# Batch 3's residual turned by transposing transfers instead of TensorE, with every step of the kernel in a new order

## The chip, the cores and the metric

The kernel runs on one core of a Trainium2 chip. The metric is the time of one execution in microseconds (us) on the device. A core has TensorE (PE in the profile; its weight loads are PEld), VectorE (DVE), ScalarE (ACT), GpSimd (POOL) and SyncE (SP), which here issues all transfers that the kernel asks for. Each engine runs its own instructions in the order in which they were written, and waits for others by semaphores.

## The reference

Eight batches of 576 positions, 8 heads of 64 channels. An attention part makes x from q, k and v, and a mixing part makes the output from x. Cut to what is computed:

```python
# attention: two terms, added
q_d, k_d, v_d = means over 4 neighbouring positions        # 576 -> 144 positions
out_up = repeat(softmax(q_d @ k_d.T / 8) @ v_d, 4)          # coarse, all 144 x 144
mask = abs(i - j) < 4
out_local = softmax(where(mask, q @ k.T / 8, -1e9)) @ v     # fine, a band of 7
x = (out_up + out_local), heads side by side                # (8, 576, 512)
# mixing
theta = x @ w_theta
zr, zi = x * cos(theta), x * sin(theta)
y = w_tok_r @ zr + w_tok_i @ zi                             # over positions
u = x + y
return u + maximum(u @ w_ch, 0)                             # (8, 576, 512)
```

## The kernel before

All matmuls are in bfloat16 with sums in float32. The work of a batch is cut into small steps, each a Python function of a batch and a piece, with a two-letter name. `ORDER` is a string of 1223 words written out ahead of time; the kernel goes through it and emits one step for each word. The first two letters name the step, the rest says where it goes: PSUM banks as digits for TensorE's steps, an engine for copies (`v` VectorE, `a` ScalarE, `g` GpSimd), a staging buffer for loads. The batch and the piece are not in the word: every step takes its next one from a fixed sequence (`STEPS`). After each word `pin()` ties every new instruction to the one before it on the same engine, so the words are the order of each engine's queue, and of SP's.

One batch goes like this. Loads of q and k (`lq`, `lk`) and of v (`lv`, `lw`, two halves of a chunk) go into 14 staging buffers `st`; `cq`, `ck`, `cv` cast them. TensorE turns q and k (`tp`, line 304) and `ev` (317) evicts them to `qT`, `kT`. `kd`, `qd` (323, 331 and on) make the coarse sums. `ps` (483), `ex` (491), `mk` (502), `po` (512), `nm` (520, 521) are the band: scores, exponentials, the mask, products with v, division. `sd` (427), `ed` (438), `pv` (405), `vd`, `nd` (448, 453), `xn` (458, 459), `xd` (467), `xc` (471) are the coarse part. `xt` (531) turns the band's result and `xa` (537) adds both into `xT`, which holds x with channels on the partitions.

`th` (548) multiplies 128 positions of x by `w_theta`, `cs` (553, 554) takes cosine and sine, `tt`, `ct` (560, 565, 566) do so for the last 64 positions. `xm` (587) turns x back for `zz` (594), which makes z; `zt` (569) with `zp`, `zc` or with the transfer `dz` (573) makes the tail of z. `mx` (610) is the mixing over positions, nine matmuls for one piece of 128 channels by 288 positions, and there are eight pieces to a batch; `ua` (615) adds x and gives `uT`. `ch` (635) multiplies by `w_ch`, `rl` (640) takes the maximum with zero and adds the residual `ur`, which is u with positions on the partitions, and `st` (644) stores. `ut`, `dt` (647), `ht`, `rt` (656) and the stores at 661 do the last 64 positions for two batches at a time.

The weight over positions comes in by `lb`, `cb`, is turned by `wp` (275) and copied to `WT` by `wc` (279); no `mx` can run before the last `wc`. `wm` words put matmuls on zeros into TensorE's queue (715). `te` and `ts` switch ScalarE's table between exponential and sine (720).

The residual `ur` is made in one of two ways. For the batches in `RPE` TensorE transposes it, `up` (624), and `uc` (627) copies it out of PSUM. For the others four transposing transfers `du` (619) do it, one for each block of 128 channels, on SP's queue and into the same buffer:

```python
def du(b, dc, w):
    nc.sync.dma_start_transpose(out=ur[b % 2][:, :, P * dc:P * dc + P], in_=uT[b % 2][:, dc, 0:512])
def up(b, c, w):
    ps = at["up", b, c] = bank16(w)[:, 0:DM]
    for dc in range(4):
        nc.tensor.transpose(out=ps[:, P * dc:P * dc + P], in_=uT[b % 2][:, dc, P * c:P * c + P], identity=ident)
def uc(b, c, w):
    COPY[w](out=ur[b % 2][:, c, :], in_=at.pop(("up", b, c)))
```

`uT`, `ur`, `xT`, `z` exist twice, and a batch takes the one of its parity.

Of the kernel before, what the change touches and what calls it, by code (L numbers as in the profile page):

```python
# [58 lines left out]
cqg lq7 lk8 lk9 tp45 cqg kcg kcg x12 lqa eva lqb kdg cvv kca cka wm62 tp67 lkc x13 lkd cvv eva ckv wm13 pv01 cqv lq0  # L59
la2 cqg lb1 tp45 qdv eva wm22 tp23 eva wm65 ps67 kdg vdv lq3 qdv ckg cka ps45 cag ex wm25 sd23 ex lb4 ed cbg lk5 sd01  # L60
cqg ps67 mkv ed po45 nm po23 nd45 nd01 la6 nm la7 xn xn lk8 mkg tp23 cag po45 ex xt6 po01 cqa eva la9 lqa mkg caa xd7
lqb ckg xca ckg nm tp23 nm xt4 xt5 lbd cag lbc cbg lb2 xt7 xa cqg lb1 eva lb0 cbg lb3 lb6 tp01 xa po23 th4 xa xm5 xa
lv7 cqg nm cbg th6 lw xt7 cbg th2 lv5 xm3 evv cbg ts cs tp01 lv8 lv9 cs cbg xa tt4 zz cs xm5 wp6 wp2 zz lw lw wp3 lw
lv4 lw cbg lqa zz ct lqd eva qdg ztv wp7 cba th4 wcv zp5 lkb xm6 wcv lkc kdg wcv wp2 wp3 wcv zcv wp0 wcv wp1 cs wp7
wca wcv ps45 lk2 lk1 wcv wcv ps23 te ex qdg ps01 lq0 zz kdv cva ex mx7 mx6 mx4 cvg ua sd23 cvg cvg mkv lc3 ex po01 ua
sd67 ed ed mkv mx5 ua nm po23 ua po01 cvg pv67 nm nm mkg vda mx4 ua po23 lq6 cqg po67 nd01 nm nd45 mx2 up3 xn lq7 ckg
xn cqg lk5 cka nm tp01 xd4 lk8 up5 uca eva xcv xt3 ucv lk9 tp67 cka xt4 xt0 ua ckg xt1 kdg lv4 xa xa xa mx5 xa eva lva
tp23 ua th4 xt0 lw xa evv cqg th5 xm1 lvb lcd lqc tt0 lw lk1 lv2 lv0 lw ts cs lw xm4 cqg cs tp67 ckg cqg th2 xm3 th5
ct lw cka zz tp01 cs qdg zz cs xm2 evv ztg lc6 lc5 zp4 mx6 ccg zz qdg zcv zz eva cvg mx7 ps45 te ex ua ps23 ua ckg kdv
ex mkv ps01 mx6 lq7 mx7 po45 sd23 ex lq8 lk3 kdg ed cvg sd01 cqg ckg ua lk4 lq9 mx6 tp23 mkv lva lw lvc lw nm ua tp45  # L70
up7 cvg mkv cvv ed mx0 eva cvg pv23 ccg ua ucv eva po67 po45 ua nm up1 nm vda ccg ccg ch0 nd67 lq1 xn nd23 lkb cqg cqa
tp45 uca qdg xn mx1 xd2 xt3 eva ps67 rl lq0 ua po45 xcv kdg qdg ps01 ch2 xa ckg ex mkg nm rl mx3 ps67 cqg lv2 cka po45
ex ua sd01 lkd xt2 ckg ex nm mx3 xt4 xt5 xa up2 ua cqa cqg tp67 cvv ed up3 xa evv uca th0 xa lv6 xt1 up2 xa lw th4 xm6
ucv ts cs uca th5 cvg lq5 ckg po01 cvg zz cs nm po23 xm7 cs ch6 nm tt4 tp01 lw ct tp23 th5 rl mkg ch4 lq7 zz st eva
evv rl po67 sd01 cs cqg cvg ztg po23 ch5 nm nm rl ch4 lv8 lw te ed cvg st pv67 vda zp0 zca lk4 cka lk3 lk1 tp23 cqa
mkg ckg lq9 lqb rl qdg lva lw xm1 eva ckg utg lv0 zz lw xm5 ch4 nd67 lvc zz xn lw nd01 mx5 lvd xn mx6 st ps23 rl lv2
ua po01 kdg nm ps45 ua mx7 lk5 ex xd0 cqa xt1 ex up6 ua xcv ucv lk6 kdv tp23 cqg utg mx0 tp45 qdg xa ua eva sd67 xt2
lv8 xt3 ch1 eva xa mkg ed xa th0 mkv rl cvg lk3 lw xt6 xt7 xa xa lw lk1 cvg th2 mx1 ua ts cs xm3 cvg tt0 zz th6 st lq4
cs cvg cka po45 dt cvg ckg ct po23 th7 mx1 ztg lk7 cs lvb nm pv45 cs ckg po67 cqg kdg lw nm ua sd23 mx0 cvg nm te ed
zp1 tp67 vdv zcv ht2 tp45 xm1 rt lw ua lq9 mx3 eva zz ps67 eva ua lva qdg po45 nm ex ps01 lq0 ex xm2 up3 zz lqc nd67  # L80
uca lvd tp45 cqa xm2 qdg xn nd01 zz mx3 cka cka xn mx2 xd0 up1 lk2 lv6 kdg st ua mx3 cqa mkv lw uca xcv eva tp67 xt0
up1 lk5 ua ua cva ucv xt4 xa mx5 st xa st eva ps23 mkg sd01 qdg po67 lw ed ua nm lv3 xt4 mx5 xt6 cva mx7 po01 ua ex
# [675 lines left out]
```

## Time and profile before

| | |
|---|---|
| Time, median of 3 runs | 236.6 us (235.68 to 238.39) |
| The profiled execution | 236.41 us, its span 234.7 us |
| Mean granted TensorE clock | 0.997 |
| Busy: TensorE, its weight loads | 223.5, 155.7 us |
| Busy: VectorE, ScalarE, GpSimd | 187.6, 159.7, 143.9 us |
| HBM read, written | 33.98, 9.44 MB |
| Start of the first `mx` | 40.62 us |

Everything below is from that one execution. Its span runs from the first to the last instruction, 1.7 us less than the time. A busy TensorE is not TensorE at its peak: the ends of its matmuls are modelled, so small waits can hide in busy time. In a group's row stand the line, the engine, what it writes and reads, the shapes, the count, then busy us and the mean ns of one, and the idle time ahead of it with what ended it. In the order of time stand the start, the duration and the instructions merged there.

### The profile page before, as it was taken

The page shows a single profiled execution, that of the slowest core. Times are in us where ns is not written, and L with a number is a line of the kernel's source. Part 1 is how long each engine was busy: PE and PEld are TensorE (multiplying, and loading weights), DVE is VectorE, ACT ScalarE, POOL GpSimd, SP SyncE. Part 2 cuts the span into 40 slices and gives each one's busy share as a digit, 9 for nine tenths or more (in the row PEclk, how much of TensorE's full clock was granted, in tenths as well). Part 3 has the DMA queues.
Part 4 walks back from the last instruction along what each step waited for, and adds up shares of the span by engine and source line. Part 5 has one row for each costly group of instructions (what it writes and reads, how often), then busy time and mean ns, then how long its engine had stood idle before and what let it go on. Part 6 is the DMA issues. An engine that isn't in the chain of part 4 may idle for free.

```text
span 234.7 us, 8524 instructions
## 1 busy us (share of the span) xinstructions
PE 223.5 (95%) x3500; PEld 155.7 (66%) x3500; DVE 187.6 (80%) x377; ACT 159.7 (68%) x239; POOL 143.9 (61%) x190
## 2 busy tenths in 40 slices
PE   7998899999999699999999999899999999999992
PEld 3555767687787466786688757676676665577740
DVE  5169997999898689888799869969898879466472
ACT  2389898669987779869987796859889358510000
POOL 7858999809999995983874628794598310100000
PEclk9999999999999999999999999999999999999998
DMA  6999979996959999999986206996967357674477
GB/s 196 383 392 386 287 163 276 391 244 143 290 162 250 243 345 212 224 224 244 287 183 173 61 0 141 292 236 139 127 155 169 73 124 197 91 221 109 110 226 244
DMA packets 76647, 49.35 MB, mean 210 GB/s; under 512 B 61120, under 2 KB 61120, under 8 KB 76608
## 3 DMA queue, kind: packets, MB, share of 16 engines
q1 hardware_dynamic: 76608, 48.81, 81.4%
q8 instruction: 27, 0.44, 0.8%
q14 instruction: 12, 0.10, 0.2%
HBM read 33.98 MB, written 9.44 MB: 185 GB/s over the span
## 4 chain that ended last, share of the span: by engine, by line
PE 85%; DVE 8%; issue 3%; DMA 2%; ACT 1%; SPq 0%; DVEq 0%
PE PS L610 29%; PE PS L635 12%; PE PS L548 10%; PE PS L304 5%; PE PS L531 3%; PE PS L512 3%; PE PS L715 3%; PE PS L587 2%; PE PS L483 2%; DMA z<-zT 2%; PE PS L275 2%; DVE tmp L521 2%; PE PS L448 2%; PE PS L624 2%; PE PS L652 1%
## 5 line engine op out<-in xcount | busy, mean ns | idle before, releaser
L610 PE MATMUL PS<-WT,z 128*128 128x288 bf16 x576 | 77.9, 286 | 0.4 <-DMA z<-zT 0.4
L610 PEld LDWEIGHTS <-z 128*128 128x128 bf16 x576 | 54.3, 98 | 16.0 <-DMA z<-zT 0.7
L615 DVE TENSOR_TENSOR uT<-PS,xT 128x288 bf16<-128x288 f32 x64 | 28.8, 452 | 12.4 <-PE PS L610 11.9
L548 PE MATMUL PS<-wth,xT 128*128 128x512 bf16 x128 | 32.2, 379 | 0.0
L635 PE MATMUL PS<-wch,uT 128*128 128x512 bf16 x128 | 31.1, 379 | 0.0
L569 POOL TENSOR_TENSOR zT<-xT,cst 128x512 bf16<-128x512 bf16 x7 | 8.1, 1153 | 35.9 <-ACT cst L566 27.6
L521 DVE TENSOR_TENSOR tmp<-PS,rl 128x512 bf16<-128x512 f32 x40 | 27.6, 691 | 1.4
L502 POOL TENSOR_TENSOR pm<-pm,band 128x1024 bf16<-128x1024 bf16 (+1 forms) x14 | 25.1, 1792 | 5.5 <-ACT pm L491 5.5
L537 DVE TENSOR_TENSOR xT<-PS,xdT 128x464 bf16<-128x464 f32 (+1 forms) x40 | 24.0, 628 | 4.5 <-PE PS L531 2.3
L640 DVE SCALAR_TENSOR_TENSOR osb<-PS,ur 128x512 f32<-128x512 f32 x32 | 21.8, 684 | 5.2 <-PE PS L635 4.9
L491 ACT ACTIVATE pm<-PS 128x1024 bf16<-128x1024 f32 (+1 forms) x24 | 20.4, 880 | 6.4 <-PE PS L483 6.4
L553 ACT ACTIVATE cs<-PS,pihc 128x512 bf16<-128x512 f32 x32 | 22.1, 692 | 3.0 <-PE PS L548 2.8
L331 POOL TENSOR_TENSOR two<-kT 128x580 f32<-128x580 bf16 x13 | 15.0, 1154 | 9.4 <-ACT kT L317 6.6
L720 ACT ACT_TABLE_LOAD x15 | 19.2, 1283 | 0.3
L635 PEld LDWEIGHTS <-uT 128*128 128x128 bf16 x128 | 11.9, 98 | 11.1
L554 ACT ACTIVATE cs<-PS 128x512 bf16<-128x512 f32 x32 | 19.2, 600 | 0.0
L594 DVE TENSOR_TENSOR z<-PS,cs 128x1024 bf16<-128x1024 bf16 x24 | 16.0, 681 | 2.4 <-PE PS L587 2.1
L548 PEld LDWEIGHTS <-xT 128*128 128x128 bf16 x128 | 11.2, 98 | 9.8 <-DVE xT L537 0.4
L438 ACT ACTIVATE pd<-PS 128x864 bf16<-128x864 f32 x16 | 13.8, 888 | 5.6 <-PE PS L427 5.6
L331 POOL TENSOR_TENSOR two<-qT 128x576 f32<-128x576 bf16 x13 | 14.9, 1148 | 4.3 <-ACT qT L317 4.0
L397 POOL CAST v_w<-st 128x512 bf16<-128x512 f32 x26 | 16.2, 647 | 0.0
L531 PE MATMUL PS<-ident,tmp 128*128 128x116 bf16 (+1 forms) x160 | 13.9, 215 | 2.1 <-issue 2.0
(116 smaller groups left out, 435.8 us busy)
## 6 DMA issues: line engine op xcount, KB each, us to landing
st<-in_k_dram SPq DMA_DIRECT2D x32, 288.0 KB, 5.3
st<-in_q_dram SPq DMA_DIRECT2D x32, 288.0 KB, 5.9
st<-in_v_dram SPq DMA_DIRECT2D x70, 128.0 KB, 5.0
out_dram<-osb SPq DMA_DIRECT2D x32, 256.0 KB, 3.0
st<-in_v_dram SPq DMA_DIRECT2D x4, 288.0 KB, 3.4
st<-in_moe_w_tok_r_dram SPq DMA_DIRECT2D x4, 288.0 KB, 6.3
st<-in_moe_w_tok_i_dram SPq DMA_DIRECT2D x4, 288.0 KB, 6.1
st<-in_moe_w_theta_dram SPq DMA_DIRECT2D x4, 256.0 KB, 7.2
```

What stands on the lines that cost most here:

```text
L331: nc.gpsimd.tensor_tensor(out=t, in0=src[:, :, 0:2], in1=src[:, :, 2:4], op=ALU.add)
L491: nc.scalar.activation(out=pm[(3 * b + u) % NPM][:, :, 0:n].rearrange("p e c j w -> p e (c j w)"), in_=at.pop(("ps", b, u))[:, :, 0:4 * W ...
L502: EW[w].tensor_tensor(out=t, in0=t, in1=m, op=ALU.mult)
L521: nc.vector.tensor_tensor(out=tmp[(NCH * b + c) % NTMP].rearrange("p g (j d) -> p g j d", d=D), in0=ps[:, :, :, 0:D], in1=r.unsqueeze(3).t ...
L531: nc.tensor.matmul(out=ps[:, kk::2, STEP * g:STEP * g + OWN[n]], lhsT=t[:, g, P * kk:P * kk + P], rhs=identw[:, :, lo:lo + OWN[n]], start= ...
L537: nc.vector.tensor_tensor(out=xT[b % 2][:, :, CH * c:CH * c + cnt].rearrange("p e (m j) -> p e m j", j=4), in0=at.pop(("xt", b, c))[:, :, ...
L548: nc.tensor.matmul(out=ps, lhsT=xT[b % 2][:, dc, P * c:P * c + P], rhs=wth[:, dc, :], start=(dc == 0), stop=(dc == 3))
L553: nc.scalar.activation(out=t[:, 0, :], in_=ps, func=AF.Sin, bias=pihc, scale=1.0)
L610: nc.tensor.matmul(out=ps, lhsT=z[b % 2][:, j, P * dc:P * dc + P], rhs=WT[:, j, cols], start=(j == 0), stop=(j == 8))
L615: nc.vector.tensor_tensor(out=uT[b % 2][:, dc, cols], in0=at.pop(("mx", b, i)), in1=xT[b % 2][:, dc, cols], op=ALU.add)
L635: nc.tensor.matmul(out=ps, lhsT=uT[b % 2][:, dc, P * c:P * c + P], rhs=wch[:, dc, :], start=(dc == 0), stop=(dc == 3))
L640: nc.vector.scalar_tensor_tensor(out=o, in0=at.pop(("ch", b, c)), scalar=0.0, in1=ur[b % 2][:, c, :], op0=ALU.max, op1=ALU.add)
```

## The change

Two things change. `RPE` loses batch 3, so the kernel emits `du` four times for it and no `up` and `uc`. And the whole `ORDER` is another one, of 1221 words. All other code is the same.

```diff
-RPE = (0, 1, 2, 3)
+RPE = (0, 1, 2)
 ZPE = (0, 1, 2, 3)
...
 ORDER = """
-l10 l11 c1g c1g k0 l12 lk3 l14 ckg c1v lk5 wm0k t101 c1g e1a kcg wm24 t123 e1a lq6 wm45 x12 cva ckg x13 cva x10 cvv
...
+l10 l11 c1v c1g wm0i t101 l12 l13 c1v c1a e1v wm22 t123 e1v wm47 x12 x13 x10 x11 x14 lk4 k0 kcg kca lq5 lk6 kcg cka
...
```

VectorE's queue, from the first mask on. Names carry the number of the buffer: `pm` are the masked scores, `rl` and `tmp` belong to `nm`, `rd` and `xdn` to `xn`. Before:

```order
L502 TENSOR_TENSOR pm_83<-pm_83,band 128x1024
L520 RECIPROCAL rl_93<-PS 128x8
L521 TENSOR_TENSOR tmp_87<-PS,rl_93 128x512
L520 RECIPROCAL rl_94<-PS 128x8
L521 TENSOR_TENSOR tmp_88<-PS,rl_94 128x512
L458 RECIPROCAL rd_97<-PS 72x8
L459 TENSOR_TENSOR xdn_95<-PS,rd_97 72x512
```

And in the changed kernel, a little later in the same stretch, after batch 0's four first `xa`:

```order
L537 TENSOR_TENSOR xT_101<-PS,xdT_99 128x4x116 x4
L502 TENSOR_TENSOR pm_85<-pm_85,band 128x2x256
L502 TENSOR_TENSOR pm_86<-pm_86,band 128x1024
L502 TENSOR_TENSOR pm_83<-pm_83,band 128x1024
L520 RECIPROCAL rl_93<-PS 128x8
L521 TENSOR_TENSOR tmp_91<-PS,rl_93 128x512
L520 RECIPROCAL rl_93<-PS 128x8
L521 TENSOR_TENSOR tmp_92<-PS,rl_93 128x512
L520 RECIPROCAL rl_94<-PS 128x8
L521 TENSOR_TENSOR tmp_87<-PS,rl_94 128x512
```

The third mask of batch 0 and two of batch 1 (`pm_86`, `pm_83`), which GpSimd or a later place had, and batch 1's `nm` (`tmp_92` and on) have moved ahead of batch 0's sines.

VectorE's queue again, at the copies of the transposed weight (`WT`), ahead of the first `mx`. `z_103` is z of batch 0, `z_104` of batch 1, `xT_101` and `xT_102` are x of the two. Before:

```order
L317 COPY kT_63<-PS 128x2x576
L537 TENSOR_TENSOR xT_101<-PS,xdT_99 128x4x112
L594 TENSOR_TENSOR z_103<-PS,cs_105 128x1024
L594 TENSOR_TENSOR z_103<-PS,cs_106 128x1024
L594 TENSOR_TENSOR z_103<-PS,cs_107 128x1024
L569 TENSOR_TENSOR zT<-xT_101,cst 128x512
L279 COPY WT<-PS 128x576 x4
L582 COPY z_103<-PS 128x512
L279 COPY WT<-PS 128x576 x4
```

In the changed kernel:

```order
L537 TENSOR_TENSOR xT_102<-PS,xdT_100 128x4x116
L569 TENSOR_TENSOR zT<-xT_101,cst 128x512
L594 TENSOR_TENSOR z_103<-PS,cs_107 128x1024
L594 TENSOR_TENSOR z_103<-PS,cs_108 128x1024
L537 TENSOR_TENSOR xT_102<-PS,xdT_100 128x4x112
L594 TENSOR_TENSOR z_104<-PS,cs_105 128x1024
L279 COPY WT<-PS 128x576 x6
L594 TENSOR_TENSOR z_104<-PS,cs_106 128x1024
L279 COPY WT<-PS 128x576 x2
```

The last copies of the weight now come behind all of x of batch 1 and two pieces of its z.

SP's queue in the changed kernel, around three of the four added transfers (`ur_115` is the odd batches' residual, `uT_113` their u; `st_127<-k_tm_76` is a transposing load step of batch 7's k; the rows on line 349 load v, on 288 q and k, on 644 and 661 store):

```order
L644 DMA out_dram<-osb_119 128x512
L619 DMA_TRANSPOSE ur_115<-uT_113 128x4x128
L308 DMA_TRANSPOSE st_127<-k_tm_76 128x9x128
L288 DMA st_128<-in_k_dram 128x576
L619 DMA_TRANSPOSE ur_115<-uT_113 128x4x128
L661 DMA out_dram<-osb_122 64x512
L349 DMA st_132<-in_v_dram 64x8x64 x2
L619 DMA_TRANSPOSE ur_115<-uT_113 128x4x128
L308 DMA_TRANSPOSE st_136<-q_tm_79 128x9x128
```

Before, no row of line 619 with `uT_113` stood in this part of the queue; the loads and stores did, in another sequence.

More of the change, by code (lines that the diff above doesn't have):

```diff
@@ L57 @@
 ORDER = """
-l10 l11 c1g c1g k0 l12 lk3 l14 ckg c1v lk5 wm0k t101 c1g e1a kcg wm24 t123 e1a lq6 wm45 x12 cva ckg x13 cva x10 cvv
[L59 to L82, printed above, removed]
@@ new lines @@
+nm po01 nm cag vda la3 lb4 lb6 lb5 lb0 cag mkg tp23 nd67 po45 xn lq7 xt0 xt1 eva kdg xa nd23 xm6 lb8 xt7 caa lb9 xn
+th0 nm xd2 xcv cbg xa th3 lba xm4 tt2 ts cs xa zz lbb lbc lqd lk2 po01 cqg th5 xt7 xt6 cbg cs th3 lk1 nm xa zz xm0 th1
+cbg cbv cbg cbg cbg cbg cs ct xm2 lk3 xt7 cs xa cs th5 ztv zz zz cs th6 xm4 zp3 cs xm1 wp0 xa lq4 zca lq7 xm5 zz wp2
+wp7 wp4 wcv wcv wcv wcv cbg wp6 wp0 wp3 lq6 wca lv5 lv8 cqa cka tt2 wcv wcv zz ct wp4 lw wcv wp7 wcv th6 lv9 ckg cqg
+tp01 xm4 ckg lk0 zz cs lw evv tp23 mx5 lw qdv lva lvb ztg cqa ua mx0 lw eva tp67 mx1 ua lw mx0 lqc lq1 eva ps23 qdg zz
@@ new lines @@
+lw cs cva zz xm2 zz ch0 ch4 ua lv6 rl cqg rl kdg ch1 sd67 te ed ckg ps23 po45 ztv cka ch0 rl nm ex mx1 tp45 rl eva xm0
+lqc ua zz tp67 tp23 cvg lq9 lka up1 uca ch0 eva mx4 cvg evv lk0 rl cvg qdg mkg zp5 po23 zca ua sd67 nm lw lvb po01 mx4
+pv23 ed ps67 cqa nm ua vdv ckg ps01 ex lw xt5 mx4 ua nd67 nd23 xn ex xn up4 uca up0 lq4 qdg mx1 up4 xd2 ucv ckg ua
+tp67 ucv xcv cqg eva kdg xt3 mx4 sd01 po67 xa ua xa nm mx2 ua cvv lv2 th3 lkd mkg cqg lw tp45 cvv ed lv1 mkg st lv3 lw
+st xt2 cvg lw xt6 lk5 xa xa cvg cvg cqa mx7 ch2 ua st po01 ts cs rl ps67 eva nm sd45 ch3 lk8 rl ckg te ed mx2 ua kdg
@@ new lines @@
+ex lka xt3 lv7 po01 po45 cka pv67 st mx2 nm nm ua xa tp01 vda nd45 tp67 nd23 eva th0 xn xn eva po45 po67 nm nm mkg
+po23 th1 utv tt4 nm ch5 st ts cs lk0 xd0 up6 xcv ct lqc up4 cqa xt7 lq9 ztv xa xt2 xa ckg th0 uca xt3 xt6 cs zp7 lq4
+cqg cqg qdg xm1 lv6 lw xa qdg zz lv2 th2 ucv xa xm3 cs xt0 rl cva up1 cs zz ch4 cka lqb xa th6 lk1 st kdg dt xm5 cqa
+lv3 lw tp23 zz cs zcv rl lw th0 uca xm5 zz cs tt6 lw xm7 cvv ct ch1 ht0 rt cvv cvg ztg zz tp45 st lvd eva lw lv5 mx6
+lw xm0 zz eva ps23 ua sd45 mx7 te ed ss ex mx0 ps45 dz ua rl cvg ckg ckg ps67 pv23 ex mkv ua ch1 utg xm0 ex zz vda rl
@@ new lines @@
+tp45 kdv tp67 up0 mx2 mx1 ucv eva sd45 lq8 lk9 eva ua po67 ua po23 mx0 lv4 st th1 ed du lw qdg nm lqc lq7 mkg nd45 cvv
+lva mx6 lw lkb xm7 lk3 ua ts cs nm ua mx0 nd23 zz lv6 xn lqd xn lv2 st lw ch1 mx4 cqa kdg cqa lw ua ps67 rl po23 mkg
+ps01 ua nm te ex ex cvv mx5 xd4 mx2 ckg ua qdg po67 ua st ckg nm po01 xca nm cvg du sd45 xt3 mx2 xt6 mx7 xt0 xa ed dk0
+ckg mx1 ps45 lk1 xa ua du mkg xa ua cvv cva sd23 ex cqg mkg ed ua po67 th0 ts cs nm pv45 po23 sr nm lv5 lw po67 mx1
+xt2 mx3 ckg xt0 xa th2 evg du nm vda ua nd45 th1 xa xm0 nd67 utg ua xn cqg tt3 th4 cs ct dk9 st dk8 xm5 cs xn xm2 zz
@@ new lines @@
+ch3 zz kdg ztg xd5 dkb zz ch0 lvc lw dz dt rl evg lva xt1 ch2 xt3 xm6 lw lv3 lw ch7 xcv xa xa cs evg zz xt1 du th3 du
+du mx6 evg cs rl cvg rl mx0 xa rl kdg mkg qdg po45 ua nm du ua ps23 ps67 lv4 qdg mx1 mx0 te ex cvg mx2 xt3 ua lw ps45
+mkv ua ua ex po67 nm sd01 cvg mx2 utv ex st st st xa cva xt6 du mx7 ua po45 sd23 xa mkg ed nm po01 ed ht6 ua nm cva st
+dx rt ch4 po23 rl pv01 vda mx5 ch4 tt0 nm dx nd67 dx ts ct rl nd23 th4 dx xn mkg ua ztg th6 du xt5 ch7 cs po01 xn st
+st cs du zz po23 zz xd4 xca th6 utg nm xt0 rl xa xt1 cs xa ch4 dz nm xt5 ch7 th0 zz xt6 du xa ch2 sr th1 xa cs xa zz
@@ L98 @@
+th0 tt3 ct mx5 rl dx cs cs ua st dx st ch3 mx6 mx1 mx0 ua ua st ztg dx th1 ss dx ht6 cs ua mx0 ch1 rl mx7 zz mx4 mx5
+rl rl zz zz ua ua zz dz st mx0 mx7 mx2 ua ua st du dt ua rt du st ua rl du sr du mx3 ua ua mx2 mx3 ua du mx2 mx0 utg
+ch1 ua ua ua ch0 st ss du rl du du st rl ch3 utg ch2 rl rl ch1 rl ch0 st dt st ch3 ch1 ht2 rl rl rl st st st st st rt
+ss sr
 """
```

25 lines of the change are left out of this document (10 added, 15 removed).

## The prediction

> **What bounds the kernel now.** I read the page's engine line and chain first, then the busy time of each engine in stretches of 10 us, then the chain in order of time.
>
> ```profile
> PE 223.5 (95%) x3500; PEld 155.7 (66%) x3500; DVE 187.6 (80%) x377; ACT 159.7 (68%) x239; POOL 143.9 (61%) x190
> PE 85%; DVE 8%; issue 3%; DMA 2%; ACT 1%; SPq 0%; DVEq 0%
> ```
>
> TensorE is busy for 95% of the span and carries 85% of the chain that ends last. VectorE's 8% sits in a few places, which the stretches show (columns: PE, PEld, DVE, ACT, POOL, granted clock, DMA share, GB/s):
>
> ```profile
> 10.00:20.00 10.00, 9.52 (x164) 5.91 (x165) 6.21 (x11) 8.47 (x12) 6.14 (x11) 1.00 1.05 394
> 20.00:30.00 10.00, 8.58 (x234) 6.50 (x223) 9.26 (x19) 8.91 (x12) 10.00 (x14) 1.00 0.96 316
> 30.00:40.00 10.00, 10.00 (x146) 6.98 (x146) 8.73 (x18) 9.16 (x16) 9.61 (x14) 1.00 0.90 206
> 40.00:50.00 10.00, 9.88 (x253) 7.46 (x241) 9.81 (x20) 6.71 (x12) 6.30 (x10) 1.00 1.08 343
> 50.00:60.00 10.00, 10.00 (x133) 7.86 (x131) 9.48 (x18) 8.78 (x15) 6.95 (x9) 1.00 0.75 179
> 70.00:80.00 10.00, 9.62 (x247) 6.96 (x244) 8.98 (x21) 8.03 (x13) 9.61 (x12) 1.00 1.04 234
> 80.00:90.00 10.00, 8.36 (x125) 6.02 (x126) 7.58 (x15) 7.15 (x13) 7.62 (x10) 1.00 1.14 302
> 150.00:160.00 10.00, 9.06 (x154) 6.63 (x153) 7.74 (x15) 6.89 (x13) 9.57 (x12) 1.00 1.18 238
> 200.00:210.00 10.00, 9.59 (x78) 6.27 (x77) 5.36 (x10) 4.06 (x8) 1.15 (x1) 1.00 0.61 155
> ```
>
> Two regimes. From 20 to 60 us VectorE is as full as TensorE: 9.26, 8.73, 9.81 and 9.48 us of every 10, 93% on average. From 60 us on TensorE alone decides, and loses little: the four last rows above are the ones in which it idles, 0.38 + 1.64 + 0.94 + 0.41 = 3.4 us in all. So an order can gain at most 3.4 us after 60 us, and it can gain or lose freely before. The chain in order of time gives the landmarks and the price of TensorE's steps (start, us, what):
>
> ```profile
> 30.61 0.86 PE PS L548 x4
> 40.62 3.41 PE PS L610 x27
> 55.02 0.86 PE PS L548 x4
> 57.17 0.47 PE PS L560 x16
> 96.02 0.45 PE PS L587 x8
> 208.11 14.33 PE PS L610 x117
> ```
>
> A theta projection (`th`) is 0.86 us, a mixing group (`mx`, nine matmuls) 14.33/13 = 1.10, a `tt` 0.47, a group of four transposes (`xm`, and `up` is alike) 0.45/2 = 0.22. The first `mx` starts at 40.62, the first `th` of batch 1 at 55.02.
>
> **What the change removes and adds.** For batch 3 it removes four `up` groups and their four copies, and adds four transposing transfers (`du`) on SP's queue. Their rows (the transfers' by the line's own view, ns min/median/max):
>
> ```profile
> L624 PE MATMUL PS<-ident,uT 128*128 128x128 bf16 x64 | 6.2, 219 | 0.0
> L627 ACT COPY ur<-PS 128x512 bf16<-128x512 bf16 x10 | 6.0, 604 | 6.7 <-PE PS L624 6.7
> L619 SPq DMA_TRANSPOSE ur<-uT x16: 1191/1238/1925, 159.1 to 223.0; - x16
> DMA to landing us min/median/max: 2.4/2.5/4.2
> ```
>
> TensorE is the bound where they stood, so its 4 x 0.22 = **0.9 us come off**. The four copies (0.60 each on ScalarE, less on VectorE) come off engines that idle a fifth of the time or more there: 0. A transfer holds SP for 1.24 us, 5.0 us for the four, with a landing of 2.5 us. What is queued behind them on SP are v and q/k loads of batches 6 and 7 and stores; `du30` comes some 8 us of TensorE work after the second of the two `ua` it needs, so it waits for nothing. Its reader, the first `rl` of batch 3, comes 28 us of such work after `du30` and about 7 after `du33`, against a landing of 2.5 to 4.2: that work covers it and I take 0. Without the cover the price is the 5.0 us of issue by which the loads behind are late.
>
> [...]
>
> **What the new order moves.** Counting the words by engine: eight v casts leave GpSimd (five to ScalarE, three to VectorE), one table switch of each kind leaves ScalarE, and there are 53 warm-up matmuls for 46, all in the start, where TensorE waits anyway. None of these engines is the bound, so the totals are worth 0 by themselves. What counts is the start. The old order goes to its first `mx` with batch 0 alone; the new one first takes batch 1 through attention and to its projections too. Ahead of its first `mx` it has 4 `th`, 4 `xm`, 1 `tt` and 1 `xt` (0.2, four matmuls) more than the old order had done at 55.02, and lacks the 7 `mx` and 2 `up` that the old one had done: 3.4 + 0.9 + 0.5 + 0.2 - 7.7 - 0.4 = 3.1 us less. So the **break-even** is a first `mx` at 55.02 - 3.1 = **51.9 us**; each us later costs one.
>
> When can it start? The last copy of the transposed weight (`wc`) must be done, and between the first mask and that copy VectorE's queue now holds 5 masks, 10 `nm`, 4 `xn`, 2 `xc`, 10 `xa`, 6 `zz`, 1 `zt`, 1 weight cast and 8 `wc`, where the old order held 1, 5, 2, 0, 5, 3, 1, 0, 8. Prices, from start to start where they run back to back, else the groups' means:
>
> ```profile
> 21.62 0.95 DVE L502 TENSOR_TENSOR pm<-pm,band 128x1024 bf16<-128x1024 bf16 x1
> 23.31 0.69 DVE L521 TENSOR_TENSOR tmp<-PS,rl 128x512 bf16<-128x512 f32 x1
> 24.14 0.69 DVE L521 TENSOR_TENSOR tmp<-PS,rl 128x512 bf16<-128x512 f32 x1
> 25.00 0.69 DVE L459 TENSOR_TENSOR xdn<-PS,rd 72x512 bf16<-72x512 f32 x1
> 25.83 0.69 DVE L459 TENSOR_TENSOR xdn<-PS,rd 72x512 bf16<-72x512 f32 x1
> 28.12 2.27 DVE L537 TENSOR_TENSOR xT<-PS,xdT 128x464 bf16<-128x464 f32 x4
> 198.56 1.28 DVE L594 TENSOR_TENSOR z<-xx,cs 128x1024 bf16<-128x1024 bf16 x2
> L502 DVE TENSOR_TENSOR pm<-pm,band 128x1024 bf16<-128x1024 bf16 x7 | 6.4, 917 | 0.0
> L502 DVE TENSOR_TENSOR pm<-pm,band 128x512 bf16<-128x512 bf16 x3 | 4.2, 1389 | 0.0
> L279 DVE COPY WT<-PS 128x576 bf16<-128x576 bf16 x8 | 3.3, 450 | 1.2 <-PE PS L275 1.2
> L569 DVE TENSOR_TENSOR zT<-xT,cst 128x512 bf16<-128x512 bf16 x1 | 0.8, 755 | 0.0
> ```
>
> Masks 4 x 0.92 + 1.39 = 5.1; `nm` 10 x 0.83 = 8.3; `xn` 4 x 0.83 = 3.3; `xa` 10 x 0.57 = 5.7; `zz` 6 x 0.64 = 3.8; `wc` 8 x 0.41 = 3.3; `zt` 0.8; the two `xc` and the weight cast, copies of a like size, are estimated at 0.5 each from the 0.45 mean of `wc`: 1.5. Sum **31.8 us**. The first mask began at 21.62; what the new order puts ahead of it (three more evictions and a sum) falls where VectorE was busy for only 6.21 of 10 us, so I keep 21.6. A VectorE that never waits is done at 53.4, 1.5 us past break-even; at the 93% of its densest stretches it needs 34.2 us, 55.8, 3.9 past. The new queue gives it more that is independent (two batches), so I take 96%: 33.1 us, 54.7, **+2.8 us**. Below 1.5 only a mask that starts earlier or masks that are cheaper would help.
>
> The mask price is the soft one:
>
> ```profile
> 42.57 0.68 DVE L502 TENSOR_TENSOR pm<-pm,band 128x1024 bf16<-128x1024 bf16 x1
> 148.39 2.13 POOL L502 TENSOR_TENSOR pm<-pm,band 128x1024 bf16<-128x1024 bf16 x1 [2.59 <-ACT pm L491]
> 149.07 1.74 DVE L502 TENSOR_TENSOR pm<-pm,band 128x512 bf16<-128x512 bf16 x1
> ```
>
> A full mask took 0.68 us once, a half one 1.74 beside a mask on GpSimd. [...] At 0.68 for all five the sum would be 1.7 us less, at 1.74 for all 3.6 more; the means lie between, and I keep them.
>
> Loads do not decide the start, although ten 128 KB loads of v now go ahead of the weights:
>
> ```profile
> 8.10 1.02 SPq L288 DMA_DIRECT2D st<-in_k_dram  x2
> 16.29 0.33 SPq L241 DMA_DIRECT2D st<-in_moe_w_theta_dram  x1
> st<-in_moe_w_theta_dram SPq DMA_DIRECT2D x4, 256.0 KB, 7.2
> ```
>
> The 13th transfer was issued at 8.10 and the 24th at 16.29, 0.75 us each. The last theta load is now the 36th: 25.3, landed at 32.5. The first `th` reuses a bank that VectorE empties some 17 us into the queue above, at about 38. Cost 0.
>
> After the start I charge **+0.8 us**: by the order, VectorE's work ahead of batch 3's first `th` was 3.9 us less than TensorE's, now 0.5 (sums of the same prices), so waits for it are somewhat likelier; bounds 0 and another 3.4, as much as TensorE idles there today.
>
> **Sum.** The profiled execution took 236.41 us (span 234.7), 0.2 under the median of 236.6. 236.41 - 0.9 + 2.8 + 0.8 = 239.1; I forecast **239.1 us**, 1.1% above the median, its own range 237.0 to 242.8 from the bounds above (1.5 and 0, 3.9 and 3.4).
>
> **Rivals.** (a) *The idle time after 60 us goes, and VectorE keeps up in the start.* The worst wait of SP's queue speaks for it, and a gap of TensorE that nothing explains:
>
> ```profile
> SPq L573 <- POOL v_w L397: 13.2, 1, 13.2
> 81.64 0.23 PE L531 MATMUL PS<-ident,tmp 128*128 128x116 bf16 x1 [2.02 <-issue]
> ```
>
> SP stood 13.2 us behind GpSimd before `dz` of batch 4, with all loads behind it, and TensorE's stall at 150 to 160 us follows; GpSimd now has eight casts less. Against: TensorE idled only 3.4 us, and the 2.0 need not vanish in another order. It needs GpSimd's queue to be what delayed SP and the start at 1.5: 236.41 - 0.9 + 1.5 - 3.4 = 233.6 us, faster. (b) *The transfers take the cover.* Four more at 1.24 us of SP among the loads of batches 6 and 7; from the point where a load lands later than its cast is due, casts, transposes and attention slip by up to 5.0 us. With the start as forecast and 3 of the 5: 242.1. Against: 14 buffers of prefetch, and today's 13.2 us stop cost under 1 us. (c) *Only TensorE's sum counts*: 236.41 - 0.9 = 235.5; this needs VectorE's 31.8 us to shrink below 30.3, which the rows do not give.
>
> **Numbers.** Forecast 0.54, (a) 0.26, (b) 0.13, (c) 0.07. A difference of 1% is about what a measurement of this kernel can tell from none; 1% above the median is 239.0, so I split the forecast's 0.54 into 0.33 slower and 0.21 within 1%; (a) is faster, (b) slower, (c) the same. Faster 0.26, same 0.28, slower 0.46. The range 233.2 to 242.8 takes in (a), (b) and the forecast's own.
>
> **What would show it.** Right: the first `mx` at 54 to 56 us, VectorE at 9.4 or more of every 10 us from 22 to 54 us, the last `wc` just ahead of that `mx`; no wait of TensorE or VectorE on `ur`; SP's wait at `dz` of batch 4 shorter. Wrong: a first `mx` at or before 52 us, or TensorE idling under 1 us or over 5 between 60 and 230 us.

## The result, and the profile after

| kernel | median us | lowest to highest | runs |
|---|---|---|---|
| before | 236.14 | 235.25 to 238.39 | 4 |
| changed | 247.13 | 243.48 to 249.96 | 4 |

The ratio is 1.040 (95% interval 1.032 to 1.048): **4% slower**, where 1.1% was forecast (239.1 us, range 233.2 to 242.8). The direction was right; the size lies outside the range. The profiled execution of the changed kernel took 249.96 us (span 248.2) at a mean granted clock of 0.982; it and the one of 247.54 us, also at 0.982, are left out of the ratio, while the shortest, 243.48 us, had 0.996, as high as the profile before (0.997), and was still 7.3 us above the median before.

The page of the changed kernel: the engine line, the granted clock in 40 slices, the chain that ended last.

```profile
PE 227.2 (92%) x3461; PEld 157.6 (63%) x3491; DVE 193.4 (78%) x378; ACT 155.4 (63%) x240; POOL 140.4 (57%) x177
PEclk9999976999999999999999999999999999999998
PE 62%; DVE 14%; POOL 8%; issue 7%; DMA 3%; SPq 2%; ACT 1%; DVEq 0%; POOLq 0%; ACTq 0%
```

TensorE carried 85% of the chain and now carries 62%; VectorE, GpSimd and "issue", time in which an engine waited for nothing that the profile shows, share the rest. The second row shows something that the old page did not have: a granted clock below full speed, 0.7 and 0.6 in the sixth and seventh slices (31 to 43 us). The busy times of the same stretches that the prediction read (PE, PEld, DVE, ACT, POOL, granted clock, DMA share, GB/s):

```profile
20.00:30.00 10.00, 8.59 (x239) 6.39 (x240) 9.52 (x17) 9.19 (x11) 9.16 (x13) 1.00 0.89 215
30.00:40.00 10.00, 6.13 (x153) 3.54 (x154) 6.76 (x12) 5.03 (x9) 9.63 (x12) 0.72 0.68 238
40.00:50.00 10.00, 9.52 (x173) 6.66 (x175) 8.73 (x20) 8.71 (x16) 6.57 (x10) 0.94 0.93 307
```

From 30 to 40 us TensorE is busy for 6.13 us of 10 instead of all ten, at a mean clock of 0.72, and VectorE, which was to be full there, has 6.76. TensorE's own rows in order of time tell what happened:

```profile
31.30 0.46 PE L483 MATMUL PS<-qT,kT 64*64 64x64 bf16 x33
32.12 0.25 PE L483 MATMUL PS<-qT,kT 64*64 64x64 bf16 x7 [0.36 <-DVE xT L537]
35.12 0.32 PE L483 MATMUL PS<-qT,kT 64*64 64x64 bf16 x8 [2.75 <-issue]
37.13 1.46 PE L715 MATMUL PS<-warm 128*128 128x512 bf16 x3
```

In the middle of one `ps` step of batch 1, eight matmuls before its end, TensorE stopped for 2.75 us and waited for nothing that the profile shows. The next eight matmuls read the same `qT` and `kT`. Then three warm-up matmuls took 1.46 us (0.82 in the rows of new_start below). The clock by stretches of 2 us:

```profile
34.00:36.00 2.00, 0.55 (x9) 0.47 (x11) 1.38 (x2) 0.46 (x1) 2.00 (x3) 0.61 0.44 163
36.00:38.00 2.00, 2.00 (x21) 0.58 (x19) 0.71 (x2) 0.65 (x2) 2.00 (x4) 0.50 0.10 27
38.00:40.00 2.00, 1.68 (x42) 0.99 (x41) 0.78 (x3) 0.85 (x2) 1.86 (x3) 0.50 0.75 210
```

Half clock from 34.4 us, while TensorE still stood, until 41.2 us. The first `mx`, from the chain in order of time, and the VectorE rows that the start was priced by (the masks, the last `wc`):

```profile
61.30 2.21 PE PS L610 x18
22.19 2.16 DVE L502 TENSOR_TENSOR pm<-pm,band 128x1024 bf16<-128x1024 bf16 x2
32.53 2.85 DVE L502 TENSOR_TENSOR pm<-pm,band 128x512 bf16<-128x512 bf16 x3
59.14 0.46 DVE L279 COPY WT<-PS 128x576 bf16<-128x576 bf16 x1 [0.41 <-PE PS L275]
```

First `mx` at 61.3 us, 9.4 past the break-even of 51.9. Behind 60 us TensorE idles more than before too (the changed kernel first, then before, both up to the last matmuls):

```profile
60.00:241.00 181.00, 173.83 (x2638) 1.00 0.75 178
60.00:230.00 170.00, 166.60 (x2583) 1.00 0.79 184
```

181 - 173.83 = 7.2 us against 3.4. And from the end of the last matmul to the end of the span it is 248.2 - 241.8 = 6.4 us, before 234.7 - 230.2 = 4.5. Together, against before: 9.4 (start) - 0.9 (`up`) + 3.8 (idle) + 1.9 (end) = 14.2, where the spans differ by 13.5.

The largest of the later waits, in GpSimd's rows and TensorE's:

```profile
176.44 1.15 POOL L569 TENSOR_TENSOR zT<-xT,cst 128x512 bf16<-128x512 bf16 x1 [5.87 <-ACT cst L566]
177.54 2.19 POOL L314 COPY qT<-st 128x1152 bf16<-128x1152 bf16 x1
179.67 2.20 POOL L314 COPY kT<-st 128x1152 bf16<-128x1152 bf16 x1
181.81 2.19 POOL L314 COPY qT<-st 128x1152 bf16<-128x1152 bf16 x1
191.86 0.26 PE L427 MATMUL PS<-qd,kd 64*64 64x144 bf16 x4 [1.65 <-POOL qd L337]
```

GpSimd stands 5.87 us behind `zt`, then copies batch 7's turned q and k three times at 2.2 us (the old order gave it two of the four copies, the new one all four), then makes the coarse sums for which TensorE waits. The end, in SP's rows and VectorE's:

```profile
234.04 3.86 SPq L619 DMA_TRANSPOSE ur<-uT  x3
239.21 0.69 DVE L640 SCALAR_TENSOR_TENSOR osb<-PS,ur 128x512 f32<-128x512 f32 x1 [1.29 <-DMA ur<-uT]
242.82 0.69 DVE L640 SCALAR_TENSOR_TENSOR osb<-PS,ur 128x512 f32<-128x512 f32 x1 [0.96 <-DMA out_dram<-osb]
```

VectorE waits for the residual of batch 7 and for `osb` buffers whose stores left late.

### The profile page after: what moved, and what is told of

Read it like the earlier page. It is cut to its first block, busy times and chain, and to the rows that moved or that the text cites. A ratio compares the mean times of both kernels' runs of the same rounds, so it can differ in the third digit from the quotient of the medians.

```text
span 248.2 us, 8448 instructions
## 1 busy us (share of the span) xinstructions
PE 227.2 (92%) x3461; PEld 157.6 (63%) x3491; DVE 193.4 (78%) x378; ACT 155.4 (63%) x240; POOL 140.4 (57%) x177
## 4 chain that ended last, share of the span: by engine, by line
PE 62%; DVE 14%; POOL 8%; issue 7%; DMA 3%; SPq 2%; ACT 1%; DVEq 0%; POOLq 0%; ACTq 0%
PE PS L610 21%; PE PS L548 7%; PE PS L635 7%; PE PS L304 4%; PE PS L715 3%; PE PS L531 2%; PE PS L512 2%; POOL two L331 2%; PE PS L483 2%; PE PS L275 2%; POOL qT L314 2%; DVE tmp L521 2%; PE PS L587 2%; DVE xT L537 2%; DVE z L594 2%
## 5 line engine op out<-in xcount | busy, mean ns | idle before, releaser
L635 PE MATMUL PS<-wch,uT 128*128 128x512 bf16 x119 | 30.6, 379 | 1.0 <-issue 0.3
L548 PE MATMUL PS<-wth,xT 128*128 128x512 bf16 x112 | 30.2, 379 | 1.1 <-issue 0.3
L569 POOL TENSOR_TENSOR zT<-xT,cst 128x512 bf16<-128x512 bf16 x5 | 5.8, 1154 | 29.6 <-ACT cst L566 29.6
L297 POOL CAST k_tm<-st 128x576 bf16<-128x576 f32 x23 | 16.4, 719 | 4.0 <-DMA st<-in_k_dram 4.0
L331 POOL TENSOR_TENSOR two<-qT 128x576 f32<-128x576 bf16 x12 | 14.2, 1183 | 7.2 <-ACT qT L317 6.9
L317 ACT COPY kT<-PS 128x1152 bf16<-128x1152 bf16 x13 | 14.6, 1122 | 4.8 <-PE PS L304 4.7
L720 ACT ACT_TABLE_LOAD x13 | 16.7, 1283 | 0.2
```

What stands on the lines that cost most here:

```text
L331: nc.gpsimd.tensor_tensor(out=t, in0=src[:, :, 0:2], in1=src[:, :, 2:4], op=ALU.add)
L548: nc.tensor.matmul(out=ps, lhsT=xT[b % 2][:, dc, P * c:P * c + P], rhs=wth[:, dc, :], start=(dc == 0), stop=(dc == 3))
L635: nc.tensor.matmul(out=ps, lhsT=uT[b % 2][:, dc, P * c:P * c + P], rhs=wch[:, dc, :], start=(dc == 0), stop=(dc == 3))
```

## The experiments

Steps are numbered by their place in the order: 1223 in the old, 1221 in the new. Where a kernel joins two orders at step n, it does the first n steps of one and then what is left in the order of the other; banks and staging buffers that were taken were renamed. Where ORDER has a line less, line numbers are one lower (L618 for L619). Ratios are to before on the same chip, with the 95% interval.

### The parts of the change, one at a time

**rpe_only**: the edit without the new order.

```diff
-RPE = (0, 1, 2, 3)
+RPE = (0, 1, 2)
-up30 uc30 up31 uc31 up32 uc32 up33 uc33   (where they stood)
+ua31 du30 ... ua33 du31 ... ua35 du32 ... ua37 du33
```

> The old order with only the first edit: batch 3's four `up` and `uc` taken out, its four `du` put in, each right behind the second `ua` that it needs. If the transfers are hidden and TensorE is the bound, 0.9 us less than the kernel before: 235.2 to 236.0. If they take the cover of the loads behind them on SP's queue (four times 1.24 us), 238 to 241 and waits for casts of batch 6 and 7 loads. If the edit is what made the change slow, 243 or more.

240.24 us, 1.020 (1.016 to 1.024). The waits of SP's queue (total, times, longest), SP's first row behind the longest, and a wait of TensorE that follows:

```profile
SPq L618 <- DVE xT L536: 20.3, 3, 16.7
125.62 2.63 SPq L618 DMA_TRANSPOSE ur<-uT  x1
149.28 0.30 PE L609 MATMUL PS<-WT,z 128*128 128x288 bf16 x1 [1.86 <-DMA z<-zT]
```

SP ran far ahead of the engines in the order here. A `du` behind "its" `ua` in the order reached SP long before that `ua` was done: SP stood for 16.7 us, and the loads of batches 5 to 7 with it. The edit costs by its place in SP's queue.

**new_up3**: the new order without the edit.

```diff
-RPE = (0, 1, 2)
+RPE = (0, 1, 2, 3)
-du30 ... du31 ... du32 ... du33
+up30 uc30 ... up33 uc33   (behind ua37, some 12 steps apart)
```

> The changed kernel's order with the first edit undone: batch 3's four `du` out, four `up` and `uc` in, between its last `ua` and its first `rl`, in banks that are free there. If the transfers cost nothing in the new order, TensorE's 0.9 us come back: 244 to 251 us, as wide as the changed kernel's own runs. If they are a cause of its loss, 241 or less, with SP's loads of batches 6 and 7 some 5 us earlier.

247.7 us, 1.049 (1.043 to 1.055), no faster than the changed kernel. The 4% are the order's.

**late_loads** and **ev7_act**: two places of the new order that its trace named.

```diff
 late_loads: two weight loads wait for other buffers and so go later
-la3 ... lb8      (the fourth theta load, the fifth of the transposed weight: staging buffers 3 and 8)
+la8 ... lb3
 ev7_act: two copies of batch 7's turned q and k
-ev700.g ... ev710.g
+ev700.a ... ev710.a
```

> The changed kernel with two words altered: the last load of w_theta goes to the staging buffer that is freed late (8) and a load of the token weight takes its place (3). SP's queue then stops before the fourth theta load until about 36 us instead of filling up with weights from 25 to 31 us. Theory F (TensorE's next instructions come by transfers that stand behind the loads in flight, so the 2.75 us gap in the middle of `ps` of batch 1 at 32.4 us is a wait for instructions, and the clock fell because of it): the gap at 32.4 us goes, the clock stays at 0.99 or more in every run, first `mx` at 54 to 57 us instead of 60.8, 240 to 243 us. Rival H (the gap is a wait on a result that the profile does not show): the gap stays where it is, the time stays at 244 to 250 us. Rival V (the start is VectorE's, the gap costs nothing): the gap goes and the first `mx` stays at 59 us or later.

> The changed kernel with two of batch 7's four copies of turned q and k (the two of k) moved from GpSimd to ScalarE. Theory G (a part of the loss after 60 us is GpSimd's queue: `zt` of batch 5 waits there for ScalarE, then three copies of 2.1 us, then the coarse sums that TensorE waits 2.1 us for at 190 us): those two waits at 190 us go and the time falls by 1.5 to 4 us against the changed kernel in runs of a like clock. Rival: TensorE finds the next wait behind it (batch 7's `po`, `nd`), and less than 1 us is gained.

244.99 us, 1.042 (1.036 to 1.047), and 245.33, 1.042 (1.038 to 1.046): nothing gained over the ratio of 1.040. In late_loads the stop at 32 us was 1.12 us long, with the DMA engines at a share of 0.38 at 30 to 35 us (0.98 in the changed kernel), so it came with far less in flight too, and no run shows that it is a wait for instructions, as theory F has it. In ev7_act, which does not touch the start, it was 1.19, in new_up3 0.65: it changes from run to run. The clock fell to half behind all three, for 3.4 us instead of 6.8, and the first `mx` came at 58.4, 58.0 and 57.0 us. ev7_act removed the waits for GpSimd and got this one instead:

```profile
202.17 0.58 PE L531 MATMUL PS<-ident,tmp 128*128 128x116 bf16 x8 [1.78 <-DVE tmp L521]
```

### Start against rest

**old_start** does the first 370 steps in the old order and the rest in the new one, **new_start** the first 352 in the new order and the rest in the old one (batch 3 by `up`), **more_warm** is the changed kernel with eight more warm-up matmuls.

```diff
 more_warm
-xd0 ... ps10 ... xt03
+xd0 wm43 ... ps10 wm63 ... xt03 wm22     (3, 3 and 2 matmuls)
```

> The first 370 steps in the old order, the rest in the new one (du of batch 3 kept), with 16 PSUM banks or staging buffers renamed where they were taken. If what is lost is lost at the start (the wait for instructions at 32 us, the half clock after it, VectorE's masks), the rest of the new order costs 1 to 3 us by its late waits less 0.9 saved: 236 to 239 us. Rival: the new order's rest, with its copies of batch 7 on GpSimd and its load casts, costs as much as its start: 240 to 243 us. If the rest is all of it: 245 us.

> The first 352 steps in the new order, the rest in the old one, batch 3's residual back on TensorE. If the start is what costs, first mx near 57 to 61 us and 242 to 246 us in all. If the rest costs half, 239 to 241 us. If the rest is all of it, 236 to 237 us.

> The changed kernel with eight more warm-up matmuls between 28 and 31 us (1.7 us of TensorE at full clock, 0.6 of it in gaps). If the clock fell because TensorE had little to do before 32 us, the granted clock at 30 to 40 us goes from 0.72-0.83 back to 0.95 or more and the time to 243 to 245 us; if the clock fell only because of the wait for instructions itself, the clock stays near 0.8 and the time at 246 to 248 us. [...]

243.03 us, 1.033 (1.027 to 1.039); 239.4, 1.016 (1.009 to 1.023); 243.55, 1.039 (1.031 to 1.047). So my theory that the start is most of it fell: 3.3% stay with the old start, though part of that came of the join (TensorE waited 1.47 us for v casts at 70 us and 0.53 for a cast of q at 72, and the clock was at half for 3.4 us behind them). New_start begins with the same 352 steps as the changed kernel, and its profile shows the same stop, short:

```profile
30.66 0.25 PE L483 MATMUL PS<-qT,kT 64*64 64x64 bf16 x7 [0.35 <-DVE xT L537]
31.11 0.26 PE L483 MATMUL PS<-qT,kT 64*64 64x64 bf16 x8 [0.20 <-issue]
31.30 0.82 PE L715 MATMUL PS<-warm 128*128 128x512 bf16 x3
```

```profile
36.00:38.00 2.00, 1.82 (x45) 1.51 (x44) 1.93 (x5) 1.68 (x3) 2.00 (x4) 1.00 1.07 274
```

The split is at the same matmul, 7 and 8, but 0.20 us long; the clock stays at 1.00, and the first `mx` comes at 55.7 us. So this start can come to its first `mx` at 55.7, and up to 61.3 - 55.7 = 5.6 us are the stop and the half clock behind it; warm_start, below, has neither and comes to it at 57.9, so not all of that need be theirs. In more_warm the stop doesn't show at all and the clock is 1.00:

```profile
31.41 0.58 PE L483 MATMUL PS<-qT,kT 64*64 64x64 bf16 x48
30.00:35.00 5.00, 4.37 (x130) 1.00 0.98 340
```

With neither a stop nor a fall of the clock in its profile, more_warm does not tell whether warm-up matmuls hold the clock. What it does tell is what is left without a long stop: 3.9%. In its profile the first `mx` is at 56.3, 4.4 past the break-even, and the idle time behind 60 us and the end are 1.3 us each above before: 4.4 - 0.9 + 1.3 + 1.3 = 6.1, where the spans differ by 6.4.

### Three single suspects

**new_tail** is the old order with the last 49 steps in the new one; **gp_copies** the old order with GpSimd's share of batch 7 as in the new one; **mended** the new order with more_warm's matmuls, the old last steps, and batch 7's engines as before.

```diff
 gp_copies
-ev701.a ... qd70.v ... ev710.a
+ev701.g ... qd70.g ... ev710.g
```

> The old kernel whole, but the last 49 steps (from mx73 on) in the changed kernel's order: du71, du72 and du73 stand together ahead of the stores. Theory (SP issues the three transfers one after the other, 3.9 us, the stores leave late and VectorE waits for osb): 1.3 to 2.4 us more than before, 237 to 238 us, with osb waiting for transfers in the last 8 us of the trace. Rival (the tail was long only because everything before it was late): 235.5 to 236.3 us.

> The old kernel, but the two copies of batch 7's turned q and k that stood on ScalarE, and one coarse sum of VectorE, are GpSimd's, as in the changed kernel (2.2, 2.2 and 1.8 us). Theory (they are what makes TensorE wait for the coarse sums at 190 us): 1 to 2.5 us more than before, with a wait for qd of GpSimd of 1 us or more in TensorE's rows. Rival (GpSimd has room in the old order, so only the new order's place of them counts): 235.5 to 236.3 us.

> The changed kernel with three mendings: the eight more warm-up matmuls of more_warm, the last steps (from mx73 on) in the old order, and batch 7's copies and coarse sum on the engines they had before. If the tail and GpSimd's queue cost about 2 us each, 239 to 241 us; if each mending only turns its wait into another, as ev7_act did, 242 to 244 us. Nothing says that it beats before: VectorE's masks and the late first mx stay.

236.15 us, 1.001 (0.998 to 1.005); 236.7, 1.001 (0.998 to 1.005); 244.25, 1.036 (1.031 to 1.041). The two suspects cost nothing in the old order, and curing both in the new one gains nothing, since the wait moves again:

```profile
200.08 0.58 PE L531 MATMUL PS<-ident,tmp 128*128 128x116 bf16 x8 [2.07 <-DVE tmp L521]
```

In new_tail the three `du` stand together ahead of the stores just as in the changed kernel, and VectorE waits for no `osb`: SP came to them in time. So the last steps cost nothing by themselves; that the long end of the changed kernel comes of SP being late is what its rows suggest, and no run shows it alone.

### Moving the join

**cut556**, **cut854** and **cut1054** begin the new order at those steps; **cut854_eng** is cut854 with batch 7's engines as before.

```diff
 cut854_eng
-ev701.g ... ev710.g ... qd70.g
+ev701.a ... ev710.a ... qd70.v
```

> The old order up to step 556 (ahead of batch 2's first mx), the new one behind it. old_start, with its cut at step 370, took 243.0 us. If the new order's stretch from batch 1 to 2 carries the cost (the wait at 70 us, the half clock after it), 239 to 240.5 us; if it is the part behind 560, 241.5 to 243.5 us.

> The old order up to step 854 (behind batch 3), the new one behind it, batch 3's residual by du where the new order has what is left of it. If the queues of batches 5 to 7 (GpSimd's copies, VectorE's tmp at 200 us, SP behind at the end) cost by themselves, 239 to 241.5 us; if they cost only because VectorE comes late out of the stretch before, 235.5 to 237.5 us.

> The old order up to step 1054 (into batch 5's mx), the new one behind it, batch 3's residual on TensorE. If the end of the new order costs by SP's place in it, the transposing transfers of batches 6 and 7 late, 237 to 239 us; if not, 235.5 to 236.5 us, as new_tail.

> cut854 with two copies of batch 7 on ScalarE and one coarse sum on VectorE, as the old order has them. If GpSimd's three copies of 2.2 us in a row are what makes TensorE wait at 177 us and what lets the clock fall behind it, the wait, the half clock and some 3 us go: 236 to 237.5 us. If the wait turns into one for VectorE or ScalarE, as in ev7_act and mended, 238.5 to 240 us.

| the new order from step | median us | ratio |
|---|---|---|
| 1174 (new_tail) | 236.15 | 1.001 (0.998 to 1.005) |
| 1054 | 237.15 | 1.006 (1.003 to 1.010) |
| 854 | 239.16 | 1.016 (1.009 to 1.023) |
| 556 | 243.50 | 1.036 (1.027 to 1.044) |
| 370 (old_start) | 243.03 | 1.033 (1.027 to 1.039) |
| 1 (changed) | 247.13 | 1.040 (1.032 to 1.048) |

The cost is spread: some 1% of the time for steps 854 to 1054 and 2% for 556 to 854. The first of these can be read. In cut854, TensorE's rows and its clock (stretches of 2 us):

```profile
178.93 0.33 PE L426 MATMUL PS<-qd,kd 64*64 64x144 bf16 x4 [1.65 <-POOL qd L336]
179.19 2.34 PE L609 MATMUL PS<-WT,z 128*128 128x288 bf16 x9
178.00:180.00 2.00, 1.07 (x8) 0.68 (x8) 0.76 (x2) 0.69 (x1) 1.92 (x5) 0.65 0.98 336
180.00:182.00 2.00, 2.00 (x13) 1.38 (x12) 0.43 (x2) 0.20 (x1) 2.00 (x1) 0.50 1.15 248
```

A wait of 0.60 and one of 1.65 us for GpSimd's sums, and then a mixing group takes 2.34 us instead of 1.10: the clock has fallen to half, for 3.4 us. The waits of 2.25 us cost some 1.5 us again behind them (an estimate: half of the 3.1 us at half clock from the end of the second wait on). cut854_eng: 237.18 us, 1.007 (1.003 to 1.011). With two copies and a coarse sum off GpSimd both the waits and the half clock are gone, and one of 1.28 us for VectorE's `tmp` at 193 us is left. So GpSimd's row of copies and sums is the cause of these waits in cut854, worth about 0.9% there (the two intervals overlap); in gp_copies the copies lie apart, with other work in between, and cost nothing.

The 2% of steps 556 to 854 are less clear. cut556 has the same two waits (0.55 and 1.65 us) and the same half clock at 181 to 186 us, so these do not tell the two apart. cut556 against cut854, TensorE's stretches (busy, clock, DMA share, GB/s):

```profile
90.00:100.00 10.00, 8.92 (x171) 1.00 0.36 73
110.00:120.00 10.00, 9.29 (x192) 1.00 1.07 299
```

cut854 shows 10.00 in both. With 0.19 at 100 to 110 that is 2.0 us of idle time, behind evictions of ScalarE (0.77 us for `z`, 0.63 for `qT`) for the most part; the first `mx` of batch 5 comes 4.0 us later (173.2 against 169.2). Where the other 2 us went I could not find; that stays open.

**warm_start** is new_start with more_warm's eight matmuls.

> new_start (239.4 us) with the eight more warm-up matmuls of more_warm, in whose trace TensorE had no wait for instructions at 31 us and the clock stayed at 1.00. If new_start's loss is that wait and the half clock in most of its runs, 236.5 to 238 us; if it is VectorE's late first mx alone, 239 to 240.5 us.

239.41 us, 1.014 (1.009 to 1.018). No stop, no fallen clock, and the same time as new_start, whose four executions also had a mean clock of 1.000: the price of the new start by itself is 1.4 to 1.6%, in warm_start with the first `mx` at 57.9 us behind the eight matmuls more.

### The edit where SP has room

**du_late**, **du_split** and **du23** are the old order with the edit, the `du` in other places; du23 turns batch 2 in the same way too.

```diff
 du_late
+lk73 du30 du31 du32 du33
 du_split
+lq70 du30 du31 du32 ... dz4 ... lv71 du33
 du23: RPE = (0, 1), and
+lw61 du20 du21 du22 du23 ... lq70 du30 du31 du32 ... dz4 ... lv71 du33
```

> The old order with batch 3's residual turned by transfers alone, as before in rpe_only (240.2 us), but all four du stand behind the last ua of batch 3 in the order, 37 words before the residual is read, so that SP is held for a word or two and not for 17 us. Theory (the edit saves TensorE's 0.9 us and costs only where SP is blocked): 234.8 to 236.0 us. Rival (the transposing transfers cost by themselves, by sharing queues or SBUF with the loads): 238 to 240 us. Rival (SP waits for the last ua still hold back loads of batches 5 to 7): 236.5 to 238 us.

> As du_late, but three of the four du of batch 3 stand ahead of dz4 in the order, where SP waits some 12 us for zT anyway, and the fourth behind lv71. In du_late the four stood right behind that wait and took 5.7 us of SP's time while it caught up on loads. Theory (the transfers cost SP's issue time and nothing else): 235.0 to 236.5 us, the loads of q behind them no more than 1.5 us later than before. Rival (each transposing transfer disturbs by itself, wherever it stands): 237.5 to 239 us, as du_late.

> du_split, and batch 2's residual turned by four transfers too, ahead of its first use where SP has some 12 us to spare. Theory (each batch taken off TensorE is worth 0.9 us where SP has the time): 234.0 to 235.3 us, some 0.9 below du_split's 235.7. Rival (TensorE's 0.9 us are lost again to waits for VectorE, whatever is taken off): 235.4 to 236.5 us. Rival (the loads behind the four come too late): 237 to 239 us.

du_late: 238.65 us, 1.014 (1.009 to 1.018). du_split: 235.66, 0.997 (0.994 to 1.001). du23: 235.22 against 236.08, **0.994 (0.991 to 0.998)**, the one kernel here whose interval lies below 1, by little and on one chip. SP's rows, du_late first, then du23:

```profile
139.82 1.23 SPq L572 DMA_TRANSPOSE z<-zT  x1
146.22 5.68 SPq L618 DMA_TRANSPOSE ur<-uT  x4
151.95 0.57 SPq L287 DMA_DIRECT2D st<-in_q_dram  x1
```

```profile
132.26 4.77 SPq L618 DMA_TRANSPOSE ur<-uT  x3
139.35 1.19 SPq L572 DMA_TRANSPOSE z<-zT  x1
146.73 1.26 SPq L618 DMA_TRANSPOSE ur<-uT  x1
```

In both SP can issue `dz4` at about 139 us only; in du_late it stands there from 127.8 on. There the four `du` come behind that wait and hold up the loads by 5.68 us just when SP is catching up; in du23 three of them fill the wait, and `dz4` still goes at 139.35. That is a difference of 1.6% for the same transfers (du_late against du_split, which has three `du` in the same wait and the fourth behind), by place alone.

## Why the prediction was wrong

**Four `up` off TensorE, -0.9.** Right in size only where SP has room: du_split's 0.3% is no more than the measurement can tell from nothing, du23, with twice the edit, gains 0.6%: somewhat less than 0.9 and 1.8 us. In the changed kernel nothing of it shows: new_up3 is no slower.

**The cover of the transfers, 0.** The rule failed, though not in this kernel. The step read the trace for work between `du30` and its reader and for a `du30` that waits for nothing; no `du` of the changed kernel waited longer than 1.6 us on SP. But "the price is the 5.0 us of issue by which the loads behind are late" is what du_late paid, and in rpe_only it was 16.7 us: what counts is where SP stands in time when it gets there, not how many steps lie between.

**The start, +2.8.** The queue of VectorE was priced well: 5.0 us of masks for 5.1, and the last `wc` of new_start done at 53.5 + 0.5 = 54.0, for a forecast of 54.7. The first `mx` came 1.5 us behind that `wc`, at 55.7, since TensorE, busy without a gap from 40 us on, had a `th`, an `xm` and two groups of transposes ahead of it; so without a long stop this start cost 3.8 us. The step that failed is "a VectorE that never waits is done at 53.4 ... I take 96%". It took for granted that TensorE feeds VectorE at full clock. In the changed kernel's profile TensorE stopped for 2.75 us (what it waited for is not shown), ran at half clock for 6 more, VectorE fell to 6.76 us of 10, and the start cost 9.4. In late_loads, ev7_act, new_up3 and more_warm, with a shorter stop or none, it cost 4.4 to 6.5. I had quoted the same kind of row of before, 2.02 us "that nothing explains", and used it only as hope for rival (a). The 53 warm-ups "where TensorE waits anyway" did not keep the clock up there (0.50 until 41.2 us).

**Later waits, +0.8.** The second term that failed, mis-sized: 3.8 us of idle time, above the bound of 3.4 that I gave it, and 1.9 us at the end, which had no place in the sum, together 5.7; 2.4 to 3.6 in the profiles of late_loads, ev7_act, new_up3 and more_warm. It weighs about as much as the start: with the old start the rest still costs 3.3%, about half of it from the join (an estimate from its rows: 2.2 us of waits and 3.4 us at half clock of the 7.3 by which the spans differ). I took GpSimd's total, eight casts less, as relief. The total did fall (143.9 to 140.4), but the three copies of 2.2 us that the order puts in a row ahead of the coarse sums made TensorE wait. A row of totals says nothing on a queue's order.

**The marks.** SP's wait at `dz` of batch 4 did shrink:

```profile
SPq L573 <- POOL zT L569: 4.2, 1, 4.2
```

4.2 us for 13.2, and it brought nothing: this one of rival (a)'s two premises came true, the other, a start at +1.5, did not, and SP's longest wait is now 10.5 us, at a `dt`. Of the marks of being right, VectorE at 9.4 us of every 10 from 22 to 54 us failed too: 8.4 in the changed kernel, 9.3 in new_start, as before. The mark "over 5 us of idle time between 60 and 230" is the one that was met. Rival (b)'s mechanism is real, but its place was another kernel, rpe_only, where SP stood for 16.7 us. Rival (c) needed VectorE to be quick in the start; its 235.5 is close to what du_split gives, where the start is the old one.

**What no term held.** Every idle time was counted once. In two profiles waits of 2 to 3 us cost up to about twice their length, by an estimate from the stretches at half clock: 2.25 us of waiting and 1.5 us of half clock in cut854, 2.75 and up to 3 in the changed kernel. That need not be so: behind the stop of 2.02 us in the kernel before, the clock stayed at 1.00. Waits of 0.60 and 1.65 us stood ahead of a fall in cut854, and waits of 0.55 and 1.65 ahead of none in new_up3, as the last section lists.

## What to carry to other kernels

Read a queue by when its engine gets to a step, not by how many steps lie between: a transfer that held SP for 1.2 us cost nothing measurable here where SP was waiting for something else (0.997 in du_split), and made the loads late where SP was catching up (1.014 in du_late). When an order is replaced, look for the longest run of work on a side engine ahead of something that the bound engine reads (three copies of 2.2 us here, and TensorE's wait of 1.65 us behind them); totals of engines don't show it. An idle time of the bound engine cost up to about twice its length here where its clock fell behind it (2.75 us and an estimated 3 more in the changed kernel); its length alone did not tell whether the clock fell.
